# One transfer for group 1's values and exchanged transpose copies in the opening of a linear-attention and SwiGLU kernel

## The chip, the cores and the metric

The kernel runs on one core of a Trainium2 chip. The metric is the device time of one execution in microseconds (us); a comparison takes the median of several executions. The kernel before has a median of 311.73 us over six executions, from 311.32 to 312.41.

The core has five engines that run their own instruction streams in order and meet at semaphores: PE (TensorE, matmuls, with PEld for its weight loads), DVE (VectorE), ACT (ScalarE), POOL (GpSimd) and SP (SyncE). Matmul results go to PSUM, which has eight banks of 128 x 512 float32; DVE and ACT bring them from there to SBUF. DMA transfers are issued here by SP and by POOL, and run on 16 shared DMA engines.

## The reference

`q`, `k` and `v` are float32 of shape (8, 8, 576, 64): batch, head, position, channel. The reference computes efficient attention and, on its result, a gated feed-forward block:

```
q_s = softmax(q, axis=-1)              # over the 64 channels
k_s = softmax(k, axis=2)               # over the 576 positions
kv  = einsum('bhsd,bhse->bhde', k_s, v)
a   = einsum('bhsd,bhde->bhse', q_s, kv)
x   = a.transpose(0, 2, 1, 3).reshape(4608, 512)
out = (silu(x @ w_gate) * (x @ w_val)) @ w_out     # w_gate, w_val: 512 x 1536; w_out: 1536 x 512
```

## The kernel before, in words

**Tiling.** Each of the 8 batches has 576 positions and 8 heads; the heads are worked in two groups of four, G = 0 and G = 1. A position is addressed as partition and column: 128 partitions hold two halves of 64 for two heads, and T = 9 columns hold the rest. Where the nine columns don't fit one PSUM bank they are cut by `BANKS = ((0, 5), (5, 9))` into a part of five columns and one of four (640 and 512 elements for a pair of heads, 320 and 256 for one head).

**Order.** Nothing is reordered by a scheduler: the part in question stands under `tc.manual_schedule()`, and each engine runs its instructions in the order in which the Python lines record them. Waits are put in where data or a buffer is not ready. The PSUM banks come from one pool of eight.

**The opening** (lines 352 to 452) is the attention of batch 0. Until it is through, the large matmuls of the feed-forward block have nothing to read. For one group it goes like this:

1. SP loads `q` and `k` (line 77). POOL loads `v` with a cast to bfloat16 into `v16[G]` (line 358 for group 0, line 361 for group 1, there in two pieces by `BANKS`), and behind that the slices of the two weights `wg` and `wv` (line 96), all in one queue.
2. ACT takes `exp` of `q` and `k` (`exp_of`, line 121). DVE sums over channels, inverts and multiplies (`norm_sum`, lines 135 and 140; `norm_mul`, line 149), which gives `qs`.
3. PE sums `ek` over positions (`key_sum`, line 397), and DVE inverts the sum into `kvr` (line 402).
4. PE turns `qs` (`turn_pe`, line 164: five transposes into one bank, four into another), and the two results `tp` are copied to `qt` (`turn_out`, lines 108 or 110, for ACT or DVE).
5. PE forms `kv` from `ek` and `v16` (`kv_first`, line 411: 36 small matmuls, 20 for the first five columns and 16 for the last four). `kv` is multiplied by `kvr` into `kn`: half by ACT (line 420), half by ACT or DVE (lines 422 and 424, `scale_first`).
6. PE forms the attention's output `xp` from `qt` and `kn` (`x_mm`, line 202), and ACT and DVE copy it to `xt` (`x_out`, lines 108 and 110: ACT the even heads' bank, DVE the odd heads').

`spin` puts matmuls on zeros (line 388) in PE's gaps. After the opening come twelve units of the feed-forward block for batch 0 (`m_unit`, lines 284, 291 and 293): `g_ps` and `u_ps` from `xt` and the weights, Silu on ACT, a product on DVE. The first unit takes the contraction by group, so that it can begin with group 0's rows of `xt`. From there on the kernel alternates between such units, the output matmuls (`o_mm`, line 317) and the attention of the next batches.

Of the kernel before, what the change touches and what calls it, by code (L numbers as in the profile page):

```python
# [15 lines left out]
def kernel(  # L16
# [10 lines left out]
    nc = tc.nc  # L27
# [10 lines left out]
    BANKS = ((0, 5), (5, T))  # L38
# [8 lines left out]
    def bank(name):  # L47
        return psp.tile([128, 512], FP32, tag="ps", name=name)
# [10 lines left out]
    v16 = [const.tile([128, 2, T * 64], BF16, name=f"v16_{i}", tag=f"v16_{i}") for i in range(2)]  # L59
# [5 lines left out]
    def head_ap(src, b, G, t0=0, t1=T):  # L65
        return bass.AP(
            tensor=src.tensor,
            offset=src[b, 4 * G].offset + 64 * t0,
            ap=[[T * 64, 128], [2 * HSTR, 2], [1, (t1 - t0) * 64]],
        )  # L70
# [35 lines left out]
    def copy(eng, out, in_):  # L106
        if eng is nc.scalar:
            nc.scalar.copy(out=out, in_=in_)
        else:
            eng.tensor_copy(out=out, in_=in_)  # L110
# [5 lines left out]
    def exp_of(what, b, G, pieces=((0, T),)):  # L116
        s = st.setdefault((b, G), {})
        e = s["e" + what] = at.tile([128, T, 2, 64], BF16, tag="e" + what, name="e" + what)
        src = raw[what, b, G].rearrange("p h (t d) -> p t h d", d=64)
        for t0, t1 in pieces:  # L120
            nc.scalar.activation(out=e[:, t0:t1], in_=src[:, t0:t1], func=AF.Exp)  # L121
# [21 lines left out]
    def norm_mul(b, G, pieces=((0, T),), engs=None):  # L143
        s = st[b, G]
        eq2 = s["eq"].rearrange("p t h d -> p (t h) d")
        qs = s["qs"] = at.tile([128, T, 128], BF16, tag="qs", name="qs")
        for (t0, t1), eng in zip(pieces, engs or (nc.vector, nc.vector)):
            n = 2 * (t1 - t0)
            last = eng.tensor_mul(  # L149
                qs[:, t0:t1, :].rearrange("p t (h d) -> p (t h) d", d=64),  # L150
                eq2[:, 2 * t0:2 * t1, :],
                s["rr"][:, 2 * t0:2 * t1].to_broadcast([128, n, 64]),
            )
        return last

    def turn_pe(b, G, i):
        s = st[b, G]
        if i == 0:
            s["qt"] = at.tile([128, T, 128], BF16, tag="qt", name="qt")
        t0, t1 = BANKS[i]  # L160
        tp = s["tp", i] = psp.tile([128, 1024], BF16, tag="ps", name="tp")
        for t in range(t0, t1):
            j = t - t0
            nc.tensor.transpose(  # L164
                out=tp[:, j * 128:(j + 1) * 128], in_=s["qs"][:, t, :], identity=ident
            )

    def turn_out(b, G, i, eng):
        s = st[b, G]
        t0, t1 = BANKS[i]  # L170
        copy(
            eng,
            s["qt"][:, t0:t1, :],
            s["tp", i][:, 0:(t1 - t0) * 128].rearrange("p (t c) -> p t c", c=128),
        )
# [19 lines left out]
    def x_mm(b, G, i):  # L195
        s = st[b, G]
        t0, t1 = BANKS[i]
        xp = [bank("xp") for _ in range(2)]
        for g in range(2):
            for h in range(2):  # L200
                r = slice(64 * h, 64 * h + 64)
                nc.tensor.matmul(  # L202
                    out=xp[h][64 * g:64 * g + 64, 0:64 * (t1 - t0)],
                    lhsT=s["kn"][r, g, :],
                    rhs=s["qt"][r, t0:t1, 64 * g:64 * g + 64],
                    start=True, stop=True,
                )
        return xp

    def x_out(b, G, i, xp, engs=(nc.scalar, nc.vector)):  # L210
        t0, t1 = BANKS[i]
        n = 64 * (t1 - t0)
        c0 = b * S + 64 * t0
        for h in (h for h in range(2) if engs[h] is not None):
            copy(engs[h], xt[:, 2 * G + h, c0:c0 + n], xp[h][:, 0:n])
# [137 lines left out]
    with tc.manual_schedule():  # L353
# [3 lines left out]
            kd.append(load("k", k, 0, G))  # L357
        d = nc.gpsimd.dma_start(out=v16[0], in_=head_ap(v, 0, 0))
        tc.add_manual_dep(d.ins, kd[0].ins.name, SYNC, reason="order of loads")
        for t0, t1 in BANKS:  # L360
            nc.gpsimd.dma_start(out=v16[1][:, :, 64 * t0:64 * t1], in_=head_ap(v, 0, 1, t0, t1))

        warm = const.tile([128, 1], FP32, name="warm", tag="warm")
        nc.vector.memset(warm, 0.0)
# [20 lines left out]
        def spin(n, after=None):  # L385
            idle = bank("idle")
            for _ in range(n):
                i = nc.tensor.matmul(out=idle, lhsT=zero[:, 0:128], rhs=zero, start=True, stop=True)  # L388
                if after is not None:
                    tc.add_manual_dep(i.ins, after.ins.name, SYNC, reason="start of the warm-up")  # L390
                    after = None
# [12 lines left out]
        def kv_first(G, t0=0, t1=T):  # L404
            s = st[0, G]
            if t0 == 0:
                s["kv"] = [bank("kv") for _ in range(2)]
            for t in range(t0, t1):
                for g in range(2):
                    for h in range(2):  # L410
                        nc.tensor.matmul(  # L411
                            out=s["kv"][g][HALF[h], 0:64], lhsT=s["ek"][HALF[g], t, h, :],
                            rhs=v16[G][HALF[g], h, 64 * t:64 * t + 64],
                            start=(t == 0), stop=(t == T - 1),
                        )

        def scale_first(G, eng1):
            s = st[0, G]
            kn = s["kn"] = at.tile([128, 2, 64], BF16, tag="kn1", name="kn1")
            nc.scalar.mul(kn[:, 0, :], s["kv"][0][:, 0:64], s["kvr"][:, 0:1])  # L420
            if eng1 is nc.scalar:
                nc.scalar.mul(kn[:, 1, :], s["kv"][1][:, 0:64], s["kvr"][:, 1:2])
            else:
                nc.vector.tensor_scalar_mul(kn[:, 1, :], s["kv"][1][:, 0:64], s["kvr"][:, 1:2])
# [5 lines left out]
        turn_pe(0, 0, 1)  # L430
        turn_out(0, 0, 0, nc.scalar)
        exp_of("k", 0, 1)
        turn_out(0, 0, 1, nc.scalar)
        norm_mul(0, 1, BANKS)
        spin(6)
        kv_first(0)
        key_sum(1)
        scale_first(0, nc.scalar)
        turn_pe(0, 1, 0)
        turn_pe(0, 1, 1)  # L440
        turn_out(0, 1, 0, nc.vector)
        turn_out(0, 1, 1, nc.vector)
        xp0 = x_mm(0, 0, 0), x_mm(0, 0, 1)
        kv_first(1, *BANKS[0])
        kv_first(1, *BANKS[1])
        x_out(0, 0, 0, xp0[0], (nc.scalar, None))
        scale_first(1, nc.vector)
        x_out(0, 0, 0, xp0[0], (None, nc.vector))
        x_out(0, 0, 1, xp0[1])
        xp1 = x_mm(0, 1, 0), x_mm(0, 1, 1)  # L450
        x_out(0, 1, 0, xp1[0])
# [153 lines left out]
```

## Time and profile before

| | |
|---|---|
| Median of six executions | 311.73 us (311.32 to 312.41) |
| The profiled execution's own time | 311.54 us |
| Its span in the trace | 309.7 us |
| PE busy | 301.6 us, 97% of the span |
| DVE, ACT, POOL busy | 52%, 47%, 10% |
| Chain that ended last, PE's share | 95% |
| Start of the first feed-forward matmul | 14.27 us after the span's start |

The time of the profiled execution is 1.8 us more than its span, which the trace does not cover. The page's fifth part names groups of instructions by line, engine and tile, with the idle time of the engine ahead of them. A matmul's record ends when its last result is out, so that records overlap: what PE can sustain is read from the starts. An instruction of DVE or ACT can likewise start some hundredths before the one ahead of it has its end.

### The profile page before, as it was taken

What the parts mean: (1) busy time and instruction counts of PE and PEld (TensorE: products, weight loads), DVE (VectorE), ACT (ScalarE), POOL (GpSimd) and SP (SyncE); (2) the same over time, 40 slices, a digit from 0 to 9 for tenths busy, and PEclk for the clock granted to TensorE, in tenths of its full rate; (3) what the DMA queues carried; (4) which work ended last, traced back from release to release, by engine and by line L of the source; (5) the groups of instructions that cost most, each with busy time, mean ns of one, the idle gap of its engine ahead of it and who ended that gap; (6) DMA issues with size and microseconds to landing.
All of it is one profiled execution on the core that took longest, in us unless ns stands there. A gap on an engine that the chain in (4) does not pass through costs nothing.

```text
span 309.7 us, 5467 instructions
## 1 busy us (share of the span) xinstructions
PE 301.6 (97%) x2182; PEld 149.8 (48%) x2182; DVE 162.0 (52%) x286; ACT 146.2 (47%) x214; POOL 32.0 (10%) x39
## 2 busy tenths in 40 slices
PE   6899999999999999999999999999999999999995
PEld 2578745554445444454445444544444444444443
DVE  3844487945754566365826492639353324433421
ACT  5743578785674375547464737455043113312300
POOL 2960021410200110002000200000000000000000
PEclk9999999999999999999999999999999999999999
DMA  7999999999347815590739352605310302020133
GB/s 273 189 193 206 271 388 390 349 212 387 91 89 211 317 33 112 135 380 15 144 74 355 100 121 61 185 0 107 72 35 0 70 11 56 3 68 8 26 71 103
DMA packets 43018, 45.78 MB, mean 148 GB/s; under 512 B 19568, under 2 KB 28272, under 8 KB 42992
## 3 DMA queue, kind: packets, MB, share of 16 engines
q1 hardware_dynamic: 34096, 39.95, 43.5%
q0 software_dynamic: 8752, 5.31, 12.0%
q8 instruction: 17, 0.28, 0.4%
q10 hardware_dynamic: 144, 0.16, 0.2%
q14 instruction: 9, 0.07, 0.1%
HBM read 37.75 MB, written 9.44 MB: 152 GB/s over the span
## 4 chain that ended last, share of the span: by engine, by line
PE 95%; DMA 2%; DVE 1%; ACT 0%; SPq 0%; issue 0%
PE g_ps L284 30%; PE u_ps L284 30%; PE o_ps L317 29%; DMA q<-in_q_dram 2%; PE kv L189 2%; PE xp L245 1%; PE o_ps L338 1%; PE tp L164 0%; DVE qs L149 0%; DVE rs L135 0%; SPq L77 0%; PE xp L202 0%; ACT eq L121 0%; ACT xt L259 0%; PE kv L411 0%
## 5 line engine op out<-in xcount | busy, mean ns | idle before, releaser
L291 ACT ACTIVATE sg<-g_ps 128x512 bf16<-128x512 f32 (+2 forms) x120 | 64.7, 554 | 133.6 <-PE g_ps L284 121.6
L293 DVE TENSOR_TENSOR hr<-sg,u_ps 128x512 bf16<-128x512 bf16 (+3 forms) x120 | 72.5, 617 | 86.2 <-PE u_ps L284 80.5
L284 PE MATMUL g_ps<-xt,wg 128*128 128x512 bf16 (+2 forms) x480 | 111.4, 358 | 0.1
L284 PE MATMUL u_ps<-xt,wv 128*128 128x512 bf16 (+2 forms) x480 | 111.3, 358 | 0.0
L317 PE MATMUL o_ps<-wo,hr 128*128 128x512 bf16 x420 | 93.9, 379 | 0.0
L284 PEld LDWEIGHTS <-wv 128*128 128x128 bf16 x480 | 46.9, 98 | 46.4
L284 PEld LDWEIGHTS <-wg 128*128 128x128 bf16 x480 | 46.3, 98 | 45.4 <-issue 0.6
L317 PEld LDWEIGHTS <-hr 128*128 128x128 bf16 x420 | 41.0, 98 | 48.6
L110 DVE COPY o_sb<-o_ps 128x512 f32<-128x512 f32 x33 | 22.4, 680 | 39.0 <-PE o_ps L317 39.0
L124 POOL CAST vb<-v 128x1152 bf16<-128x1152 f32 x14 | 17.1, 1219 | 137.5 <-DMA v<-in_v_dram 99.4
L135 DVE TENSOR_REDUCE rs<-eq 128x18 f32<-128x1152 bf16 (+2 forms) x18 | 21.7, 1214 | 12.9 <-ACT eq L121 12.9
L149 DVE TENSOR_TENSOR qs<-eq,rr 128x1152 bf16<-128x1152 bf16 (+2 forms) x18 | 22.2, 1240 | 0.1
L121 ACT ACTIVATE eq<-q 128x1152 bf16<-128x1152 f32 (+2 forms) x18 | 18.3, 1052 | 4.0 <-DMA q<-in_q_dram 4.0
L121 ACT ACTIVATE ek<-k 128x1152 bf16<-128x1152 f32 (+2 forms) x17 | 17.9, 1101 | 0.5 <-DMA k<-in_k_dram 0.5
L291 ACT ACT_TABLE_LOAD x12 | 15.4, 1283 | 0.2
L121 ACT ACT_TABLE_LOAD x11 | 14.1, 1283 | 0.2
L259 ACT CAST xt<-xp 128x512 bf16<-128x512 f32 x14 | 7.8, 587 | 4.4 <-PE xp L245 4.4
L260 DVE CAST xt<-xp 128x512 bf16<-128x512 f32 x14 | 9.0, 682 | 0.7 <-PE xp L245 0.7
L388 PE MATMUL idle<-zero 128*128 128x512 bf16 x20 | 6.4, 475 | 2.8 <-DVE rs L135 1.6
L189 PEld LDWEIGHTS <-ek 64*64 64x64 bf16 x504 | 6.3, 107 | 1.7 <-ACT ek L121 0.4
L189 PE MATMUL kv<-vb,ek 64*64 64x65 bf16 x504 | 6.7, 194 | 0.0
L245 PE MATMUL xp<-qt,kn 64*64 64x512 bf16 (+1 forms) x112 | 6.7, 292 | 0.0
(44 smaller groups left out, 66.4 us busy)
## 6 DMA issues: line engine op xcount, KB each, us to landing
q<-in_q_dram SPq DMA_DIRECT2D x16, 576.0 KB, 5.1
out_dram<-o_sb SPq DMA_DIRECT2D x70, 128.0 KB, 2.3
k<-in_k_dram SPq DMA_DIRECT2D x12, 576.0 KB, 7.9
v<-in_v_dram SPq DMA_DIRECT2D x12, 576.0 KB, 9.3
wo<-in_moe_w_out_dram POOLq DMA_DIRECT2D x4, 384.0 KB, 15.4
k<-in_k_dram SPq DMA_DIRECT2D x4, 320.0 KB, 8.3
k<-in_k_dram SPq DMA_DIRECT2D x4, 256.0 KB, 8.6
v<-in_v_dram SPq DMA_DIRECT2D x2, 320.0 KB, 7.7
```

What stands on the lines that cost most here:

```text
L110: eng.tensor_copy(out=out, in_=in_)
L121: nc.scalar.activation(out=e[:, t0:t1], in_=src[:, t0:t1], func=AF.Exp)
L124: return nc.gpsimd.tensor_copy(out=vbs[G][:, :, :, 0:64], in_=raw["v", b, G].rearrange("p h (t d) -> p t h d", d=64),)
L135: i = nc.vector.reduce_sum(out=rs[:, 2 * t0:2 * t1], in_=eq2[:, 2 * t0:2 * t1, :], axis=mybir.AxisListType.X)
L149: last = eng.tensor_mul(qs[:, t0:t1, :].rearrange("p t (h d) -> p (t h) d", d=64), eq2[:, 2 * t0:2 * t1, :], s["rr"][:, 2 * t0:2 * t1].to_ ...
L189: nc.tensor.matmul(out=kv[g][HALF[h], c:c + 65], lhsT=ek[HALF[g], t, h, :], rhs=vbs[G][HALF[g], t, h, :], start=(t == 0), stop=(t == T - 1),)
L245: nc.tensor.matmul(out=o[h][HALF[g], c:c + 64 * (t1 - t0)], lhsT=kn[HALF[h], g, G, :], rhs=qt[G][HALF[h], t0:t1, 64 * g:64 * g + 64], star ...
L260: nc.vector.tensor_copy(out=xt[:, 2 * G + 1, c0:c0 + 512], in_=main[G][1])
L284: nc.tensor.matmul(out=gu[a][i][:, 0:w_], lhsT=(wg, wv)[a][:, kk, ms], rhs=xt[:, kk, c:c + w_], start=(kk == 0), stop=(kk == KT - 1),)
L291: nc.scalar.activation(out=sg[:, 0:w_], in_=g_ps[:, 0:w_], func=AF.Silu)
L293: nc.vector.tensor_mul(hr[:, m, r:r + w1], sg[:, 0:w1], u_ps[:, 0:w1])
L317: nc.tensor.matmul(out=o_ps, lhsT=hr[:, m, r0:r0 + 128], rhs=wo[:, m, :], start=(m == 0), stop=(m == MT - 1),)
```

## The change

Three things are changed, all in the opening. The values of group 1 come by one transfer of 2 x 576 columns instead of two of 2 x 320 and 2 x 256, and `kv_first(1)` is one call instead of two. The copy of the second transposed part of group 0 (`turn_out(0, 0, 1)`) goes from ACT to DVE and is recorded behind `norm_mul(0, 1)`; the copy of the first part of group 1 (`turn_out(0, 1, 0)`) goes from DVE to ACT. The two halves of `x_out(0, 0, 0)` are recorded together ahead of `scale_first(1)`; before, DVE's half stood behind it.

```diff
         d = nc.gpsimd.dma_start(out=v16[0], in_=head_ap(v, 0, 0))
         tc.add_manual_dep(d.ins, kd[0].ins.name, SYNC, reason="order of loads")
-        for t0, t1 in BANKS:
-            nc.gpsimd.dma_start(out=v16[1][:, :, 64 * t0:64 * t1], in_=head_ap(v, 0, 1, t0, t1))
+        nc.gpsimd.dma_start(out=v16[1], in_=head_ap(v, 0, 1))
...
         turn_out(0, 0, 0, nc.scalar)
         exp_of("k", 0, 1)
-        turn_out(0, 0, 1, nc.scalar)
         norm_mul(0, 1, BANKS)
+        turn_out(0, 0, 1, nc.vector)
         spin(6)
         kv_first(0)
         key_sum(1)
         scale_first(0, nc.scalar)
         turn_pe(0, 1, 0)
         turn_pe(0, 1, 1)
-        turn_out(0, 1, 0, nc.vector)
+        turn_out(0, 1, 0, nc.scalar)
         turn_out(0, 1, 1, nc.vector)
         xp0 = x_mm(0, 0, 0), x_mm(0, 0, 1)
-        kv_first(1, *BANKS[0])
-        kv_first(1, *BANKS[1])
-        x_out(0, 0, 0, xp0[0], (nc.scalar, None))
+        kv_first(1)
+        x_out(0, 0, 0, xp0[0])
         scale_first(1, nc.vector)
-        x_out(0, 0, 0, xp0[0], (None, nc.vector))
         x_out(0, 0, 1, xp0[1])
         xp1 = x_mm(0, 1, 0), x_mm(0, 1, 1)
```

PE's instructions keep their order and number. The lines behind the shortened loop move up by one, and those at the end of the opening by three.

## The prediction

> **What bounds the kernel now.** I read the page first, for who is busy and what the chain that ended last is made of; then that chain in order of time for the first 15 us; then the timeline of the same stretch; then the DMA queues by stretches; and last the waits of PE over the whole span. From the page:
>
> ```profile
> PE 301.6 (97%) x2182; PEld 149.8 (48%) x2182; DVE 162.0 (52%) x286; ACT 146.2 (47%) x214; POOL 32.0 (10%) x39
> ```
>
> PE is the bound, and its idle time lies almost wholly in the opening. The waits of PE over the whole span are four, the longest first:
>
> ```profile
> PE idle L388 <- DVE rs L135: 1.6, 1, 1.6
> PE idle L388 <- DVE sel L367: 1.2, 1, 1.2
> PE kv L411 <- DMA v<-in_v_dram: 0.7, 1, 0.7
> PE xp L202 <- DVE kn L424: 0.4, 1, 0.4
> ```
>
> All are before 13.9 us. After that PE runs its feed-forward matmuls at their pace to the end, so what the opening gains or loses is carried to the end one for one, and nothing that shifts behind it matters unless it makes PE wait anew. The chain in order of time shows what leads to the first feed-forward matmul:
>
> ```profile
> 10.76 1.44 DVE qs L149 x2
> 12.20 0.05 issue
> 12.24 0.40 PE tp L164 x4
> 12.64 0.37 PE xp L202 x8
> 13.01 0.16 PE kv L411 x20
> 13.16 0.00 issue
> 13.17 0.37 PE kv L411 x16
> 13.54 0.03 issue
> 13.56 0.29 DVE kn L424
> 13.86 0.03 issue
> 13.89 0.45 PE xp L202 x8
> 14.34 0.60 PE g_ps L284 x4
> ```
>
> Up to 12.19 nothing on this chain is touched (q's transfer, exponential, sums, `qs`). After it come four transposes, eight matmuls of group 0's `xp`, the 36 of group 1's `kv`, the scaling `kn`, and group 1's `xp`. The place to look at is the break in `kv` between the 20 and the 16. In the timeline the 20 start at 12.84 and are issued within about 0.14; the 16 start only at 13.17. They need the second piece of group 1's values, issued at 8.0 with 5.1 to landing, so at 13.1. So PE stands still for about 0.19 us there, waiting for a transfer, and 13.17 is set by that.
>
> **The transfer.** The two pieces become one of 2 x 576 columns. Its issue costs POOL 0.72 (a piece) to 0.86 (group 0's), where the pair took 1.43: the weights behind it are issued 0.57 to 0.71 earlier. But the issue is not what lands late: from 9 us on the queue is backed up. The DMA queue by stretches, first 9.0 to 9.5 us (group 0's rows of 1152 bytes), then 9.9 to 11.7 us (the pieces of 640 and 512 bytes):
>
> ```profile
> q0 software_dynamic: 84, 0.10, 113.3%
> ...
> q0 software_dynamic: 490, 0.28, 124.1%
> ```
>
> Group 0's 256 packets are through at about 9.9 (252 of them from 8 to 9.9), and it landed at 6.43 + 4.6 = 11.03, a lag of 1.13. The pair's 512 packets are through at about 11.7, landing at 13.1, a lag of 1.4. The merged transfer has 256 packets of the size of group 0's. At that row's pace, 84 in 0.5 us, they take 1.52 us and are through at 11.42, so landed between 12.55 and 12.82 by the two lags. At the worst they keep the pair's bytes per us and land at 13.10 as the second piece did. Below, group 0's 4.6 from issue would give 7.29 + 4.6 = 11.89. I take 12.7, since the rows are exactly group 0's.
>
> The Trainium skill, DMA: Bandwidth & Descriptors, section "Why small descriptors are slow (HBM only)", speaks for less: a fixed cost of some 3 cycles for a packet beside its 32-byte beats. By that the pieces of 20 and 16 beats would cost 256 x (23 + 19) = 10752 cycles and the whole 256 x 39 = 9984, 7% less, an estimate that would put the landing near 12.95 and the effect of the whole change near zero; the packet rows above show more than that between the two sizes.
>
> All of `kv` now waits for the whole transfer, the 20 matmuls too, which today start at 12.84 on the first piece. If it has landed by 12.77, the 36 run from 12.84 in one go: group 0's 36 took 0.29 from first start to last start (11.07 to 11.36), so the last starts at 13.08 to 13.13 and ends, 0.19 later, by 13.32. Today it ends at 13.49. If it lands at 13.10, they start at 13.17, and the 20 cost 0.11 to 0.14 behind the landing that they don't cost now. The break-even is a landing at about 12.98.
>
> **DVE's order.** DVE runs, from the end of `qs` at 12.19: the copy of group 0's second part (512 elements), the reciprocal `kvr`, the copy of group 1's second part, DVE's half of `x_out`, then its half of `kn`. The rows that price this:
>
> ```profile
> 12.20 0.49 DVE L110 COPY qt<-tp 128x640 bf16<-128x640 bf16 x1
> 12.68 0.42 DVE L110 COPY qt<-tp 128x512 bf16<-128x512 bf16 x1
> 13.56 0.28 DVE L424 TENSOR_SCALAR kn<-kv,kvr 128x64 bf16<-128x64 f32 x1 [0.46 <-PE kv L411]
> 13.77 0.48 DVE L110 CAST xt<-xp 128x320 bf16<-128x320 f32 x1
> ```
>
> The first copy runs from 12.10 to 12.53 (today the reciprocal starts at 12.10, just ahead of the end of `qs`). The second half of group 0's `xp`, at 12.73 on PE, needs it, and `kv`, `kn` and all that follows are queued behind that matmul: 0.2 of slack. If the copy were as slow as ACT's own (0.57) it would end at 12.67, still in time. The reciprocal moves from 12.10 to about 12.45 and ends at 12.61; `kv` on PE waits for its bank at 12.84: 0.2 of slack. The copy of group 1's second part stays at 12.68, where its transposes end, until 13.10. The `x_out` half stands free at 12.90, when its matmuls end; it starts at about 13.02 (copies start 0.08 before the one ahead ends) and ends at 13.50. `kn` is queued behind it and can start at 13.41 to 13.45, where `kv` would allow 13.36. So DVE holds `kn` back by some 0.05 to 0.1, and this caps what the transfer can bring: `kn` from 13.56 to 13.41, group 1's `xp` from 13.89 to 13.74, the feed-forward from 14.27 to 14.12. That is -0.15 us.
>
> **ACT.** It loses a copy at 11.04, which ended at 11.61 just as `kv` of group 0 was ready at 11.55: nothing to gain, since `kn` would start at 11.57 instead of 11.59. It gets the 640 copy at about 12.18, after `kn`, for 0.67, done at 12.85; its half of `x_out` starts at 12.94 as now. `qt` of group 1 is not read before 13.7. These are free, covered by `kv`; uncovered they would cost 0.67.
>
> **What is late next.** The first weight slice landed at 8.71 + 5.1 = 13.81 and the first of `wv` at 9.46 + 5.2 = 14.66, where its weight load starts: no slack there today. Both move up with the queue by 0.28 or more at the rate I take, which covers the 0.15. If the transfer saves nothing, they stay, and so does the start. The fourth `g_ps` matmul, at 14.66, needs DVE's 256 copy, which ends at 14.57 today; it will end at about 14.03. ACT's Silu table load (1.28) follows its last `xt` copy and moves along.
>
> **Sum.** 311.54 - 0.15 = 311.39 for the profiled execution; it stood 0.19 under the median, so 311.58 for a median, 0.05% less. A measurement of this kernel tells about 0.2% (0.62 us) from no change; this is within it.
>
> **The rivals.** (1) *The transfer is hidden anyway or saves nothing*: landing at 13.10, `kv` 0.11 to 0.14 later, 311.85. For it: the queue is backed up and bytes, not issues, set the landing. Against it: the packet rows.
> (2) *The landing is late, and slower is the verdict.* One transfer of more bytes, of which PE needs all. The nearest large rows of this queue are the 256 KB weight slices, 6.0 and 6.6 to landing; from 7.29 that is 13.29 and 13.89, so +0.31 and +0.91 over the break-even of 12.98: 312.04 to 312.64. It decides a verdict of slower from a landing at 13.60. For it: PE's first 20 matmuls lose the early piece. Against it: those slices have rows half as long and lie deeper in the backlog; group 0's, of the very same shape, took 4.6.
> (3) *PE's clock.* The first spins start 0.43 apart, the later ones about 0.24, so PE has a slow state that it left by 6.3 us. If longer idling at 12.9 to 13.2 brought it back for as long as the first stretch lasted (3.5 us), half of that would be lost: +1.75, 313.5. Against it: the granted clock is 1.00 in every half microsecond, and PE stood idle for 1.6 us at 4.7 and still ran the next spins fast.
> (4) *More gain than DVE's order allows*, if its intervals are shorter: `kn` as early as 13.35 and ACT's half with it, -0.25 at most. No route to 0.62 shows in the profile; a median of few runs can itself stand 0.3 off, as the six show.
>
> **How the numbers follow.** The forecast case gets 0.52, rival 1 0.22, rival 2 0.12 (half of it beyond 0.62), rival 3 0.05, rival 4 0.09. The range of 311.2 to 312.1 takes in -0.25 with the runs' spread below, and the near end of rival 2 above; rival 3 and the far end of rival 2 are left out. Faster by over 0.2%: 0.12, from rival 4 and the low side of the spread. Slower: 0.06 of rival 2, 0.05 of rival 3 and 0.07 of rival 1 with the spread, 0.18. Within: 0.70.
>
> **What would show it.** Right: one `kv` run of 36 without a break from 12.84, landing before 12.8, `kn` on DVE directly behind the 320 copy at about 13.4, the first `g_ps` at about 14.12. Wrong: a wait of `kv` on the values after 12.84 (rivals 1 and 2), `xp` waiting on DVE's copy at 12.73, `g_ps` starting 0.27 apart instead of 0.14 (rival 3), or a new wait of PE behind 14.3, of which I predict none.

## The result: 0.35% slower, and what the profile after shows

The changed kernel takes 312.57 us in the median of 19 executions (311.85 to 314.16), the kernel before 311.71 in 42 (310.77 to 312.81). The ratio is 1.0035 with a 95% interval from 1.0025 to 1.0046. The forecast was 311.6, and 312.57 is outside its range of 311.2 to 312.1, on the slow side.

The 19 times are not one cluster. Five lie between 313.69 and 314.16. In four of them the mean granted clock of PE over the span is 0.994 or 0.995. In the fifth (313.84), as in the other fourteen, it is 0.998 or more, so that one high time has a cause that the record does not show. The fifteen at the higher clock have a median of 312.5. The profiled execution (313.79 us, span 311.5) is one of the four at the lower clock, so its trace shows two losses at once. The first is in the waits of PE over the whole span (who waits, for whom, us in total, times, longest):

```profile
PE idle L387 <- DVE rs L135: 1.6, 1, 1.6
PE kv L410 <- DMA v<-in_v_dram: 1.3, 2, 1.0
PE idle L387 <- DVE sel L366: 1.2, 1, 1.2
PE xp L202 <- ACT kn L419: 0.4, 1, 0.4
```

The wait for the values was 0.7 us before, all of it ahead of group 0's `kv`. It is now 1.3 us in two waits, 0.3 ahead of group 0's `kv` and 1.0 ahead of group 1's. The chain in order of time from 10 to 19.5 us (start, length, what) shows the transfer as its first link, and behind it the second loss:

```profile
7.27 6.18 DMA v<-in_v_dram
13.45 0.04 issue
13.50 0.55 PE kv L410 x36
14.04 0.30 ACT kn L419
14.35 0.04 issue
14.39 0.45 PE xp L202 x8
14.84 1.07 PE g_ps L284 x4
15.91 0.96 PE u_ps L284 x4
16.87 0.96 PE g_ps L284 x4
17.83 0.74 PE u_ps L284 x4
18.57 0.98 PE g_ps L284 x8
```

The values were issued at 7.27 and landed 6.18 later, at 13.45. The 36 `kv` matmuls then run without a break, and the first `g_ps` matmul starts 0.50 later than before. PE's timeline, first of before, then of after:

```profile
14.27 0.67 PE L284 MATMUL g_ps<-xt,wg 128*128 128x320 bf16 x4
```

```profile
14.77 1.14 PE L284 MATMUL g_ps<-xt,wg 128*128 128x320 bf16 x4
```

Then four matmuls take 0.96 us where at 18.57 eight take 0.98. The stretches show why (PE, PEld, DVE, ACT and POOL busy, each with its count, the granted PE clock, DMA share, GB/s):

```profile
11.41:14.82 3.41, 2.00 (x65) 1.12 (x62) 2.15 (x8) 2.00 (x7) 2.87 (x5) 1.00 1.51 154
14.82:18.23 3.41, 3.41 (x18) 2.11 (x16) 0.80 (x2) 2.71 (x5) 3.28 (x5) 0.50 1.65 188
```

PE was granted half its clock for 3.41 us, from about 14.8 to 18.2, just when its large matmuls began. Half of 3.41 is 1.7. The second feed-forward step's first `g_ps` starts at 18.57, before at 16.40: 2.17 later, 0.50 from the wait and 1.67 from the clock. From there nothing is added: the output matmuls at line 338 start at 305.50 against 303.31, and the span is 1.8 longer, the very end having become 0.4 shorter.

### The profile page after: what moved, and what is told of

Same layout as the page of the kernel before. It is cut to its first block, busy times and chain, and to the rows that moved or that the text cites. A ratio compares the mean times of both kernels' runs of the same rounds, so it can differ in the third digit from the quotient of the medians.

```text
span 311.5 us, 5466 instructions
## 1 busy us (share of the span) xinstructions
PE 303.3 (97%) x2182; PEld 150.3 (48%) x2182; DVE 161.5 (52%) x286; ACT 146.2 (47%) x214; POOL 31.6 (10%) x38
## 4 chain that ended last, share of the span: by engine, by line
PE 94%; DMA 4%; ACT 0%; POOL 0%; issue 0%; SPq 0%; DVE 0%
PE g_ps L284 31%; PE u_ps L284 30%; PE o_ps L317 29%; DMA v<-in_v_dram 2%; DMA k<-in_k_dram 2%; PE kv L189 2%; PE xp L245 1%; PE o_ps L338 1%; PE tp L164 0%; POOL v L358 0%; ACT xt L259 0%; PE kv L410 0%; SPq L77 0%; PE xp L202 0%; DVE o_sb L342 0%
## 5 line engine op out<-in xcount | busy, mean ns | idle before, releaser
L135 DVE TENSOR_REDUCE rs<-eq 128x18 f32<-128x1152 bf16 (+2 forms) x18 | 21.7, 1213 | 12.5 <-ACT eq L121 12.5
L121 ACT ACTIVATE eq<-q 128x1152 bf16<-128x1152 f32 (+2 forms) x18 | 18.2, 1051 | 2.8 <-DMA q<-in_q_dram 2.8
```

What stands on the lines that cost most here:

```text
L135: i = nc.vector.reduce_sum(out=rs[:, 2 * t0:2 * t1], in_=eq2[:, 2 * t0:2 * t1, :], axis=mybir.AxisListType.X)
```

## The experiments

The theories were: **(L)** the landing of the merged transfer makes the wait, and the wait makes the loss; **(C)** PE's idle time also lets the granted clock fall, which costs some 1.7 us in the executions that it strikes; and the rivals **(D)** that the exchanged copies cost the time, on DVE or ACT, and **(Q)** that what is queued behind the transfer, not the transfer's own form, makes it late. In the texts below "half clock" is an execution whose mean granted clock is 0.995 or less. Each ratio is to the kernel before on the same chip, whose medians were 311.93, 311.73 and 311.78 us in the three comparisons.

**The two halves of the change.** First the transfer alone: the kernel before with this edit only.

```diff
-        for t0, t1 in BANKS:
-            nc.gpsimd.dma_start(out=v16[1][:, :, 64 * t0:64 * t1], in_=head_ap(v, 0, 1, t0, t1))
+        nc.gpsimd.dma_start(out=v16[1], in_=head_ap(v, 0, 1))
```

> The kernel before with only the transfer of group 1's values made one; copies and recording order as before. Theory T (the late landing of the merged transfer is the whole loss): PE waits for the values up to 13.3 to 13.6 us as in the changed kernel, median 312.3 to 312.7, and some executions at 313.6 to 314.2 in which PE's clock falls to half for one stretch behind that wait. Rival R (the exchange of the copies between ScalarE and VectorE costs): no loss, 311.6 to 311.8.

Measured: 313.15 us (12 executions), ratio 1.0043, interval 1.0022 to 1.0064; 3 of 12 at half clock, the other nine with a median of 313.1. That is above the 312.3 to 312.7 that was expected, and the whole loss is here. PE's timeline (start, us, what, idle time ahead and its releaser):

```profile
12.52 0.44 PE L202 MATMUL xp<-qt,kn 64*64 64x320 bf16 x8
13.70 0.48 PE L410 MATMUL kv<-v,ek 64*64 64x64 bf16 x36 [0.74 <-DMA v<-in_v_dram]
14.59 0.45 PE L202 MATMUL xp<-qt,kn 64*64 64x320 bf16 x8 [0.41 <-DVE kn L423]
```

`kv` is released by the transfer again, at 13.70, and with the old order of the copies.

Then the exchange alone: the changed kernel with the two pieces put back (the same lines the other way round), run in two comparisons.

> The changed kernel with the values of group 1 in two pieces again; the exchange of the copies and the new order of the x_out halves stay. Theory T: the loss is gone, median 311.4 to 311.8, no execution above 313.2, and kv's 36 matmuls broken behind the 20 as before. Rival R: 312.3 to 312.7, with the loss on kn or xp behind DVE's queue.

> The exchange alone once more, the same kernel as in the second run, for the interval: by the forecast's own sum (kn 0.05 to 0.1 earlier where the values are in time) it should lie 0 to 0.3 us under the kernel before; rival R would have it 0.5 or more over.

Measured: 311.56 (12), ratio 0.9986, 0.9969 to 1.0004, and 311.55 (12), ratio 0.9993, 0.9976 to 1.0010; 1 of 24 at half clock. Neither a loss nor a gain that this measurement can tell, so D falls. The first of the two profiles, in PE's timeline, and one line of the kernel before:

```profile
12.76 0.44 PE L202 MATMUL xp<-qt,kn 64*64 64x320 bf16 x8
13.03 0.46 PE L411 MATMUL kv<-v,ek 64*64 64x64 bf16 x36
13.93 0.44 PE L202 MATMUL xp<-qt,kn 64*64 64x320 bf16 x8 [0.45 <-ACT kn L420]
14.30 0.66 PE L284 MATMUL g_ps<-xt,wg 128*128 128x320 bf16 x4
```

```profile
12.57 0.44 PE L202 MATMUL xp<-qt,kn 64*64 64x320 bf16 x8
```

From group 0's `xp` to the first `g_ps` it is 1.54 us here, where the kernel before took 12.57 to 14.27, 1.70. `kv` runs without a break, against the expectation: the values were there in time. In the second profile the distance is 1.71 (12.56 to 14.27): its last piece landed at about 13.1 again. So the 0.15 is there when the values are there in time, and only then. It is the break in `kv` that goes; that the exchanged copies have a part in it is not shown, since no profile of a kernel with the old order has the values in time.

**Is it the idle time that halves the clock?** Two edits of PE's filling alone. The changed kernel with four matmuls on zeros in the gap where it waits:

```diff
         xp0 = x_mm(0, 0, 0), x_mm(0, 0, 1)
+        spin(4)
         kv_first(1)
```

> The changed kernel with four more matmuls on zeros (0.86 us) between group 0's xp and group 1's kv, in the place where PE waits for the values. If the slow quarter of the changed kernel's executions (313.7 to 314.2) comes from PE standing idle there: no execution above 313.3, median 312.1 to 312.6, clock 1.00 from 5 us on. If the clock falls for another reason: still about a quarter of the executions near 314. If the whole loss were the clock: the median goes back to 311.7.

And the kernel before without the six that stand ahead of `kv_first(0)`, all transfers as they were:

```diff
         norm_mul(0, 1, BANKS)
-        spin(6)
         kv_first(0)
```

> The kernel before without its third group of six matmuls on zeros (ahead of group 0's kv), so that PE stands idle for 1.3 us more from 8.9 us on while nothing else is changed. If idle time of PE in the opening lets the clock fall: a part of the executions lies 1.5 to 1.9 us higher, 313.2 to 314, with a stretch of 3.4 us at half the granted clock in the first 20 us. If the clock has nothing to do with idle time: 311.7 throughout.

Measured: with four more, 312.9 (12), ratio 1.0033, 1.0018 to 1.0047, and none of 12 at half clock: the highest is 313.86 with a clock of 0.999. The median and three of the twelve lie above what was expected (312.6 and 313.3). At the rate of the same transfer without these four (10 of 43, below), twelve in a row at full clock would come by chance in about 4% of cases, so that the spins keep the clock is likely and not certain. The time is not won back: in the profile the values landed at 7.33 + 6.5 = 13.83, and the spins ran past it:

```profile
13.09 1.04 PE L387 MATMUL idle<-zero 128*128 128x512 bf16 x4
14.06 0.48 PE L410 MATMUL kv<-v,ek 64*64 64x64 bf16 x36
...
15.33 0.45 PE L284 MATMUL g_ps<-xt,wg 128*128 128x320 bf16 x2
```

`kv` started at 14.06, some 0.2 behind the landing because of the spins, and the first `g_ps` 1.06 later than before; the median is 0.97 above the kernel before. So the later start costs by itself, without C. With six fewer, 312.87 (12), ratio 1.0026, 1.0006 to 1.0045, and 7 of 12 at half clock: those seven lie from 312.45 to 313.73, the other five from 311.54 to 312.52 with a median of 311.66. No transfer was touched, so C stands without L. In that kernel the mean clock was 0.988 or 0.989 in five of the seven, twice the loss of one such stretch; none of the seven was profiled, so where the stretches lay is not shown.

**Is it the form of the transfer?** The changed kernel with group 1's values in two transfers again, but cut by pairs of heads, so that each row keeps its 1152 bytes:

```diff
-        nc.gpsimd.dma_start(out=v16[1], in_=head_ap(v, 0, 1))
+        for h in range(2):
+            src = bass.AP(tensor=v.tensor, offset=v[0, 4 + 2 * h].offset, ap=[[T * 64, 128], [1, T * 64]])
+            nc.gpsimd.dma_start(out=v16[1][:, h, :], in_=src)
```

> The changed kernel with group 1's values in two transfers again, but cut by head pair: each brings 128 rows of the full 1152 bytes, and kv needs both from its start. Theory S (what lands late is the merging into one transfer): the second lands near 13.0 us as the second piece of before does, median 311.5 to 311.9. Theory L (the long rows, not the one transfer, are slow on the slowest DMA engine): it lands at 13.4 or later, PE waits for it, median 312.3 to 312.9.

> The kernel of the fifth run once more, for the interval and a second landing: 311.3 to 311.6, landing 12.4 to 12.8 us, 0.7 or more under the changed kernel on the same chip.

Measured: 311.38 (12), ratio 0.9993, 0.9979 to 1.0008, and 311.64 (12), ratio 1.0001, 0.9989 to 1.0012; none of 24 at half clock. The loss is gone with the same rows and the same bytes. The DMA issues (KB each, us to landing) of the transfer alone (first kernel above), then of the first of these two kernels, its two halves:

```profile
v<-in_v_dram POOLq DMA_DIRECT2D x1, 288.0 KB, 6.4
```

```profile
v<-in_v_dram POOLq DMA_DIRECT2D x1, 144.0 KB, 4.7
v<-in_v_dram POOLq DMA_DIRECT2D x1, 144.0 KB, 4.9
```

The second half is issued some 0.6 us behind the first and was in by about 12.6 here, by 12.9 in the second run (expected there: 12.4 to 12.8). In the first, `kv` ran unbroken from 12.92 and the first `g_ps` stood at 14.19, 1.54 behind group 0's `xp`.

The same with both groups, four transfers:

> The changed kernel with the values of both groups in two transfers by head pair. If what shortens the landing is the smaller transfer, group 0's values land near 10.6 us too (before: 11.03), and group 1's at 12.4 to 12.7; nothing on the way to qs is shortened, so the time is that of the fifth run, 311.2 to 311.5. If group 0 lands no earlier, the shape is not what counts.

Measured: 312.02 (12), ratio 1.0015, 1.0000 to 1.0029. This went against the expectation. Group 0's values were complete only at about 11.4, against 11.03 before (and 10.5 to 11.2 in the other profiles in which `kv` waited for them), and group 1's at about 13.3; the four issues took POOL 2.31 us where the three of before took 0.86 and 1.43. PE's timeline:

```profile
11.43 0.47 PE L413 MATMUL kv<-v,ek 64*64 64x64 bf16 x35 [1.00 <-DMA v<-in_v_dram]
```

So smaller transfers are not shown to be earlier as such, though this is one profile; the second run of the two halves, at 12.9, also shows how little separates the cuts.

**Is it what is queued behind?** The changed kernel, with the first weight slice held until `qs` of group 1 is done, so that no transfer of POOL's follows the values until 12.37 us (a single execution):

> The changed kernel, but POOL issues the first weight slice only when qs of group 1 is done (about 12 us), so that nothing is queued behind the merged transfer while it runs. Its time is of no interest (the weights come late); what counts is the landing of the values. Theory B (the weights' descriptors and packets behind it, issued 0.7 us earlier than before the change, slow it): landing at 12.4 to 12.8 us. Theory I (the transfer's own rows are held up, whatever is behind): 13.3 to 14.1 us as in the three profiles with the merged transfer.

Measured: issued at 7.21, landed at about 13.1 (5.9). PE's timeline:

```profile
13.14 0.48 PE L406 MATMUL kv<-v,ek 64*64 64x64 bf16 x36 [0.20 <-DMA v<-in_v_dram]
```

That lies between the two theories. With the weights behind it the merged transfer landed at 13.45, 13.66, 13.59 and 13.83 in four profiles; without them at 13.1, still later than the halves with the weights behind them. By this one execution Q is a part of it and not the whole. (The execution took 315.71 us: the weights came late, and the clock was halved from about 16.6 to 20.0.)

**How far does it go?** The halves by heads, put behind the first slice of each weight, issued from 8.84 on:

> The fifth run's two transfers, but issued behind the first two weight slices, 1.5 us later: a late landing without any merging. If the landing alone sets the loss: landing 13.8 to 14.3 us, first g_ps 1.3 us behind it, most executions at 312.3 to 313.0 and a part 1.7 higher with the clock down. If the loss belongs to the merged transfer in some other way: 311.3 to 311.7.

Measured: 314.8 (6), ratio 1.0097, 1.0076 to 1.0119, and 5 of 6 at half clock. They landed later than expected (13.8 to 14.3), the last at about 14.57. PE's timeline:

```profile
13.86 0.21 PE L413 MATMUL kv<-v,ek 64*64 64x64 bf16 x1 [0.84 <-DMA v<-in_v_dram]
14.61 0.47 PE L413 MATMUL kv<-v,ek 64*64 64x64 bf16 x35 [0.53 <-DMA v<-in_v_dram]
16.12 1.14 PE L284 MATMUL g_ps<-xt,wg 128*128 128x320 bf16 x4
```

The first `g_ps` is 1.85 later than before. In this profile the clock was already halved from 15.22 on, so a part of the 1.85 is the clock. The one execution at full clock was not profiled; it took 313.58, 1.8 above the 311.78 of its comparison, so a landing that is late without any merging costs time by itself. The other five have the clock on top.

**Filling instead of gaining.** The exchange alone with one spin behind `kv_first(1)`, to see whether PE's short wait for `kn` matters:

> The kernel with the exchange alone (values in two pieces) with one more matmul on zeros behind group 1's kv, where PE waits 0.4 us for kn. If it hides there and keeps the clock up: median as the exchange alone, 311.3 to 311.7, no execution at 313.5 or more. If it delays group 1's xp: 0.1 to 0.3 more.

Measured: 311.74 (11), ratio 0.9996, 0.9978 to 1.0013. No difference that can be told. And the changed kernel itself once more, in the third comparison:

> The changed kernel itself once more, beside the others on the same chip, for another landing and more executions: merged transfer landing at 13.3 to 14.1 us, median 312.3 to 312.8, about a quarter of the executions 1.3 to 1.8 us higher with the clock down for 3.4 us.

Measured: 312.7 (12), ratio 1.0032, 1.0010 to 1.0054; 3 of 12 at half clock (313.95 to 314.57), the other nine with a median of 312.46. Its profile is one at full clock: `kv` is released by the transfer at 13.61, and the first `g_ps` stands at 14.89, 0.62 later than before. That agrees with 312.46 - 311.78 = 0.68.

**The account.** In the comparison of the result, the executions at full clock have 312.5 against 311.71, so the late landing is worth about 0.8 us; the first `g_ps` stood 0.50, 0.62 and 0.70 later in the three profiles of the merged transfer without added spins, and where it lands differs from execution to execution. The halved clock adds about 1.5 (the four's middle, 313.9, less 312.5) in 4 of 19; it moves the median little and the spread much. What it costs depends on where the stretch falls: one execution of the kernel before had a mean clock of 0.994 at 311.56 us, one of the exchange with a spin 0.994 at 311.91. Over three kernels with the merged transfer and no added spins (the changed kernel twice, and the transfer alone) 10 of 43 executions were at half clock; over the four comparisons with two transfers (exchange alone twice, halves by heads twice) 1 of 48, and in the kernel before itself 3 of 93. The exchange with a spin had 1 of 11, both groups in halves 1 of 12.

No version beats the kernel before: every interval that reaches below 1 also holds 1.

## Why the prediction was wrong, point by point

**What bounds the kernel** was read rightly. Each 0.1 us by which the feed-forward starts later is in the time, and no wait of PE stands behind 14.9 us in the changed kernel.

**The transfer** is the step that failed, at its sentence "I take 12.7, since the rows are exactly group 0's". The landing measured 13.45 in after, 13.66 with the transfer alone, 13.59 in the second run of the changed kernel and 13.83 with the four spins, 0.75 to 1.13 us later. The break-even of 12.98 held: the first `g_ps` follows the landing by 1.3 us (13.45 to 14.77, 13.59 to 14.89), which puts a landing for the old 14.27 at 12.97, and a landing at 12.89 gave 14.18. What failed is how the landing was built: packets "through at 11.42", by a pace of the whole queue, and a lag of 1.13 to 1.4 behind that. The transfer is only there when the last of its own packets is, and both terms came from counting whatever the queue started up to a given time. Of the 252 packets counted up to 9.9 only 234 are group 0's. By the packet records of the trace of before, group 0's last packet started at 10.59 and its landing followed 0.44 later; the pair's last started at 12.78, not at about 11.7. So the lag of 1.13 was for the most part late packets, and the size of such a tail was taken over without a look at what makes it.

In the trace of after, of all 512 packets of 1152 bytes (both groups), 75% were started by 10.80 and 95% by 11.71. But the last started at 13.07. In the half microseconds from 11.5, 12.0, 12.5 and 13.0 there started 18, 12, 6 and 1. The queue as a whole shows it too, first from 9.9 to 11.5 us, then from 11.5 to 12.0 (packets, MB, share of 16 engines):

```profile
q0 software_dynamic: 261, 0.26, 111.5%
...
q0 software_dynamic: 114, 0.04, 73.0%
```

In that second stretch the kernel before moved 0.09 MB in 242 packets. A few packets took up to 1.43 us where most took 0.107, and the last seven started one behind the other, 0.09 us apart. This reads as a few of the 16 engines being far behind the rest; the trace gives no engine for a packet, so that is a reading and not shown.

Nor is it the same in every execution. In the changed kernel's second run the whole of the packets is late and not a tail: 75% were started by 11.54, 95% by 12.74, the last at 13.17. Its queue from 9.9 to 11.5 us:

```profile
q0 software_dynamic: 164, 0.17, 90.3%
```

What the four profiles of the merged transfer with the weights behind it have in common is the end: the last packet started at 13.07 to 13.44, where the sum had 11.42, and the landing came some 0.4 behind it. With two halves the last started at 12.14 and 12.48. The worst case, "at the worst they keep the pair's bytes per us and land at 13.10", was no bound either: it too went by a mean pace. The estimate from the Trainium skill, "DMA: Bandwidth & Descriptors", section "Why small descriptors are slow (HBM only)", 12.95, was nearer than the row's 12.7 and still 0.5 short: it too counts a mean cost and no tail.

Why the merged transfer's last packets are this late, and those of two halves with the same rows less so, is not settled. The weights behind it seem to make a part of it (13.1 with them held, in one execution, against 13.45 to 13.83). The cause of the rest is open: how the packets of one transfer are dealt to the engines, against those of two, was not tried by itself.

**Rival 2** had the right mechanism and, at its near end, the right place: landing 13.29 to 13.89, 312.04 to 312.64, with 0.12. Its "against it", that group 0's transfer of the same shape took 4.6, misled. The row put forward for it, 6.0 for a 256 KB weight slice, was the nearer one: the merged transfer took 6.2 to 6.5 with the weights behind it.

**Rival 3** was given 0.05 and its price, +1.75, was nearly exact (1.67 in the trace). But it was set up as an alternative to rival 2, and it is a consequence: the wait is what makes PE idle enough. Its "against it", 1.6 us of idling at 4.7 with fast spins after, compared the length of one gap. The runs speak for what PE does over a whole stretch, and not for one gap. The stretches of 3.41 to 3.42 us ahead of a halved clock, in the profiles of after (shown above) and of the kernel with the transfers behind the weights, and a stretch of the changed kernel's second run, which kept its clock:

```profile
11.73:15.14 3.41, 1.96 (x62) 1.17 (x58) 1.70 (x5) 1.59 (x5) 3.41 (x6) 1.00 1.48 178
```

```profile
11.41:14.82 3.41, 2.33 (x103) 1.54 (x90) 2.56 (x8) 2.24 (x7) 2.83 (x5) 1.00 1.41 153
```

PE was busy for 2.00 and 1.96 of 3.41 us ahead of a fall (1.51 with the weights held), and for 2.33 where none came; the transfer alone, at 2.23, kept its clock as well. The kernel before has 2.92 there.

Why the same wait is struck in some executions and not in others can be read from the traces' clock records. Full clock is first entered at 4.2 to 5.0 us in seven of the fourteen profiles and at 9.3 to 10.2 in the other seven; before that the spins start 0.43 apart, behind it 0.22. (So the "granted clock is 1.00 in every half microsecond" of the prediction holds only from 4.49 on, where the records of before begin.) Every later change up to the last matmuls stands at a whole multiple of 3.413 us behind the first: in after 4.56, 14.80 and 18.22. Counted in stretches from these points, PE was busy for 2.01 us ahead of the fall in after, 1.89 behind the weights and 1.58 with them held, and in the stretches from 7.6 us on behind which the clock stayed, it was never less than 2.26. But the sum alone does not decide: in the seven profiles with the early start, the first stretch of full clock held only 1.71 to 1.91 us of PE (4.49 to 7.90 in before: 1.79, with the gap of 1.6), and the clock stayed. There PE ran the large matmuls on zeros, and in the opening mostly small ones; whether that is the difference was not tried.

The Trainium skill, "TensorE: Matmul & The Clock Gate", Part 1, describes a free-running window of 3413 ns that sets the clock to full or half by PE's activity; the length and the 0.50 agree with the trace. Its table, section "Why this matters for your kernels", warns of idle gaps over some 3 us. Here the trace differs: the longest gap in the stretch was 0.99 us, and the measurement decides.

**DVE's order** was right as far as the runs show it. Group 0's copy, the reciprocal, group 1's copy and the `x_out` half ran directly behind one another in after (DVE's timeline), `xp` did not wait for them, and `kn` came behind:

```profile
11.60 0.42 DVE L110 COPY qt<-tp 128x512 bf16<-128x512 bf16 x1
11.94 0.16 DVE L401 RECIPROCAL kvr<-ks 128x2 f32<-128x2 f32 x1
12.18 0.42 DVE L110 COPY qt<-tp 128x512 bf16<-128x512 bf16 x1
12.52 0.48 DVE L110 CAST xt<-xp 128x320 bf16<-128x320 f32 x1
14.07 0.28 DVE L423 TENSOR_SCALAR kn<-kv,kvr 128x64 bf16<-128x64 f32 x1 [1.07 <-PE kv L410]
```

The last line is the change's outcome in one row: DVE was ready 1.07 us before `kv`. The forecast gain of 0.15 agrees with the 1.54 against 1.70 of the two profiles with the values in time; in the changed kernel it was never reached. **ACT's** 640 copy (11.80 to 12.49) was free, as predicted.

**What is late next** held with one thing missing: a new wait on POOL. Its tenth issue, a slice of `wv`, waited 0.54 us, by the profile for the values' landing, in after and in its second run:

```profile
13.74 0.75 POOL L96 DMA_DIRECT2D wv<-in_moe_w_val_dram  x1 [0.54 <-DMA v<-in_v_dram]
```

PE never waited for that slice. The same issue waited 0.76 us with the transfer alone and 0.89 with the four spins, and not at all in the kernels with two transfers. Why an issue of weights should wait for the values is not shown.

## What to carry to other kernels

A consumer that needs all of a transfer starts when its last packet is in (here some 0.4 us after that packet's start), so count the packets of that transfer alone, and price a merged transfer from the landing of the nearest transfer of its size in the same, already full, queue, and not from the mean pace of its packets. When a change can lengthen a wait of PE in a stretch where PE is already sparsely busy, add up PE's busy time over 3.4 us around it, as a sign and not as a rule, and put the halved clock's price on the same case: the wait and the clock come together. Where single executions stand 1.5 us above their median, look at their mean granted clock before looking for a second cause; it explained four of the five highest times of the changed kernel's 19.

## What was not expected of the hardware

- The clock of PE fell to 0.50 for 3.41 us after a stretch in which PE was busy for 2.00 of 3.41 us with no gap over 0.99 us, while 1.79 us with a gap of 1.6 us kept it earlier in the kernel before; without six of the matmuls on zeros 7 of 12 executions of the kernel before had a lower mean clock, and with four more in the gap none of 12 of the changed kernel.
- One transfer of 288 KB took 6.2 to 6.5 us from issue to landing where two of 144 KB with the same rows took 4.1 to 5.0 each and were all in by 12.6 and 12.9. Cutting group 0's the same way did not bring it in earlier (11.4 in one profile, against 10.5 to 11.2 uncut).
- In after, 1.36 us lay between the start of 95% of a queue's packets of one size and the last of them (11.71 to 13.07); in the second run of the same kernel it was 0.43 (12.74 to 13.17), with the last packet as late.
